# A sparse-attention and feed-forward kernel: a new order table, half products for a third of batch 0, and queries of batches 2 and 3 loaded eight tokens to a partition

## Chip, cores and metric

The kernel runs on one core of a Trainium2 chip. The metric is device time in microseconds (us), the median of several executions. A separate, profiled execution gives the trace that this document reads.

## The reference

The inputs are `q`, `k`, `v` of shape (4 batches, 8 heads, 768 tokens, 64) and the weights of a feed-forward block, all float32. Each query attends to the keys less than 16 tokens away, and to one summary for each block of 32 tokens: the elementwise maximum of the block's keys with the mean of its values, with log 32 added to its score.

```python
k_sum = k.reshape(B, H, nb, block, D).max(axis=3)
v_sum = v.reshape(B, H, nb, block, D).mean(axis=3)
scores_l = scale * q @ k.T            # kept where |i - j| < 16
scores_s = scale * q @ k_sum.T + log(block)
a = softmax([scores_l, scores_s]); attn = a @ [v, v_sum]
h = x @ w_in                          # x: attn as (3072 tokens, 512); h: (3072, 2048)
g = h * sigmoid(beta * h)
out = g @ w_out                       # (3072, 512)
```

## The kernel before

**Tiling.** The four batches are worked one after another, and heads in four groups `g` of two (one head in each half of the 128 partitions). For a group, `kT` and `qn` hold keys and queries transposed: partition = head and feature, free axis = token. A query tile has 64 tokens. Its keys are the 96 in its window and the 24 block summaries, together one 128-column block of `kw`; so one matmul of 64 columns per head and tile gives all its scores (`scores`, L318 to L327: for a group and a half `u` of the tokens, 12 matmuls into two PSUM banks). ScalarE (ACT) takes the exponential of the 768 columns (`weigh`, `e`), VectorE (DVE) multiplies with a band mask (`mask_e`, L338), TensorE (PE) multiplies with the values (`av_mm`, L403; `ve` and `vo` are the values in two alignments, with the block means put in by `vm_all`, L377, and `spread`), and `norm` (L429, L430) divides. The result `xn` is transposed into `xT` by a DMA (`x_dma`, issued on ACT's queue).

**Feed-forward.** The hidden layer has 16 tiles `h_tile` of 128 hidden units: 4 blocks of 128 features times two halves of 384 tokens (L475), then one activation (L488). The first two tiles are opened together over three of the four feature blocks, so that the fourth block of `xT` may come late. The second product (`second_product`) makes two row tiles of 128 tokens at a time by seven half-size products instead of eight (Winograd's form of Strassen's method): `product` (L545) runs 8 matmuls of 256 columns, on operands of which some are sums that DVE makes ahead (`h_sums` of the activations, `w_sums` of the weights), and `gather` adds the parts up and stores. Batch 0 alone uses direct products (`o_atom`, L493): six row tiles of 16 matmuls with 512 columns.

**Order.** Nothing schedules the kernel automatically; every engine runs its instructions in the order in which they are written. `run(main, sides)` goes through a list of PE steps and after step `i` puts in the side steps whose position is below `i + 1`. The stages are, in order: batch 0's attention with the first half of its hidden layer; the second half; batch 0's second product beside batch 1's attention; then for batches 1, 2 and 3 the hidden layer (16 steps, with the next batch's loads, casts and transposes beside it) and the second product (21 steps, with the next batch's attention beside it). Each stage has a list of its own with hand-written positions.

**Loads.** Batches 0 and 1 load keys and queries eight tokens to a partition and turn them on PE. For batches 2 and 3, `hw_load` (L109) loads keys and queries in pieces of 256 bytes, one token of one head each, into one pool `stage` of seven buffers; GpSimd (POOL) casts them to bfloat16 (`kq_cast`, L451, a pool `nat` of five buffers), and `kq_dma` (L455) transposes them into `kT` and `qn` in natural token order. These DMAs, the value loads, `v_odd_dma` (which fills `vo` from `ve`) and most output stores wait their turn on one queue, SyncE's (SP).

The query load and the score matmul before:

```python
nc.sync.dma_start(out=f[:], in_=pair(src, b, g).rearrange("h (j p) d -> p h j d", p=P))
nc.tensor.matmul(s[:, h, j * QT:(j + 1) * QT], kw[g][h * D:(h + 1) * D, m, :], q_tile(g, h, m),
                 start=True, stop=True)
```

Of the kernel before, what the change touches and what calls it, by code (L numbers as in the profile page):

```python
# [8 lines left out]


@with_exitstack
def kernel(
# [43 lines left out]
    stage = ctx.enter_context(tc.tile_pool(name="stage", bufs=7))  # L56
    natp = ctx.enter_context(tc.tile_pool(name="nat", bufs=5))
# [48 lines left out]
    def hw_load(nm, src, b, g):  # L106
        f = stage.tile([P, 2, J6, D], f32, name=nm + "st", tag="st")
        stg[(nm, b, g)] = f
        nc.sync.dma_start(out=f[:], in_=pair(src, b, g).rearrange("h (j p) d -> p h j d", p=P))  # L109
# [210 lines left out]
    def scores(b, g, u, bg):  # L320
        s = big[bg]
        for j in range(HT):
            m = u * HT + j
            for h in range(2):
                nc.tensor.matmul(s[:, h, j * QT:(j + 1) * QT], kw[g][h * D:(h + 1) * D, m, :], q_tile(g, h, m),
                                 start=True, stop=True)
        weigh(b, g, u, s)  # L327
        if g < G - 1 or b == 1:
            mask_e(b, g, u)
# [6 lines left out]
    def mask_e(b, g, u):  # L336
        e = et[(b, g, u)]
        (nc.gpsimd if (b, g) == (1, G - 1) else nc.vector).tensor_mul(out=e.rearrange("p h (m q) -> p h m q", q=QT), in0=e.rearrange("p h (m q) -> p h m q", q=QT),  # L338
# [109 lines left out]
    def kq_cast(eng, nm, b, g):  # L448
        t = natp.tile([P, J6, 2, D], bf16, name=nm + "n", tag="nat")
        nat[(nm, b, g)] = t  # L450
        eng.tensor_copy(out=t[:], in_=stg[(nm, b, g)].rearrange("p h j d -> p j h d"))  # L451

    def kq_dma(nm, b, g):
        t = kT[g][:, W:W + S] if nm == "k" else qn[g][:]
        nc.sync.dma_start_transpose(out=t.rearrange("p (j t) -> p j t", j=J6),  # L455
                                    in_=nat[(nm, b, g)].rearrange("p j h d -> p (j h d)"))
# [13 lines left out]

    def h_part(i, k_lo, k_hi):
        t = big[(i + 2) % 3]
        for kk in range(2):
            for ki in range(k_lo, k_hi):
                nc.tensor.matmul(t[:, kk, 0:HS], w_in_sb[:, ki, i * P:(i + 1) * P],  # L475
                                 xT[:, ki, kk * HS:(kk + 1) * HS], start=(ki == 0), stop=(ki == k1 - 1))

    def h_tile(i):
        t = big[(i + 2) % 3]
        if i > 1:  # L480
            h_part(i, 0, k1)
        elif i == 0:
            h_part(0, 0, k1 - 1)
            h_part(1, 0, k1 - 1)
            h_part(0, k1 - 1, k1)
        else:
            h_part(1, k1 - 1, k1)
        nc.scalar.activation(out=h_sb[:, i, :].rearrange("p (k m) -> p k m", k=2), in_=t[:, :, 0:HS],  # L488
# [385 lines left out]
```

## Time and profile before

| | |
|---|---|
| median of 3 runs | 215.6 us (215.23 to 216.23) |
| profiled execution | 215.75 us, its span 214.0 us |
| PE busy | 201.3 us (94%) |
| DVE / ACT / POOL busy | 137.4 / 117.6 / 65.2 us |
| DMA | 85,274 packets, 34.13 MB, 73,712 packets under 512 B |

The span runs from the first to the last instruction; 1.75 us of the device time lie around it. A busy time is the union of an engine's instructions; matmuls overlap, so a group's mean duration times its count is more than its busy time, and the pace of matmuls is read from a row with many of them in a line. In a row `line engine op out<-in | busy, mean | idle before <-releaser`, the last part tells how long the engine stood idle just before these instructions and what ended that.

### The profile page before, as it was taken

Reading aid. Unit: us, or ns where it says so; the run is one execution under the profiler, and the core shown is the slowest. Engines: PE = TensorE matmul, PEld = TensorE weight load, DVE = VectorE, ACT = ScalarE, POOL = GpSimd, SP = SyncE. Lnnn points to the kernel's source line nnn. Section 1 sums busy time; section 2 is a strip of 40 time slices with the busy share of each in tenths; the row PEclk is TensorE's granted clock in tenths of the full one; section 3 lists DMA queues with packets and bytes.
Section 4 is the critical chain, followed back from the end, with each engine's and each line's share of the span. In section 5 each row is a group of like instructions: output and inputs, shape, how many; then the busy total and the mean of one; then the engine's idle time right before and its main releaser. Section 6 shows DMA issues by size and latency. Waiting matters only on the chain.

```text
span 214.0 us, 5814 instructions
## 1 busy us (share of the span) xinstructions
PE 201.3 (94%) x2414; PEld 140.0 (65%) x2419; DVE 137.4 (64%) x313; ACT 117.6 (55%) x173; POOL 65.2 (30%) x98
## 2 busy tenths in 40 slices
PE   7688999999989999999999989999999999999992
PEld 7567766665535546666877856667778866668881
DVE  5396684797476773898799623898999404465122
ACT  2366776787767106667965027778772157662220
POOL 7808991011432800434230171463301100001011
PEclk9999999999999999999999999999999999999998
DMA  6997999999949987999969999999935720000222
GB/s 117 182 223 130 190 178 189 207 206 214 199 118 206 197 258 178 219 178 198 181 158 241 184 280 193 238 205 191 155 112 72 176 103 0 0 3 0 98 101 98
DMA packets 85274, 34.13 MB, mean 159 GB/s; under 512 B 73712, under 2 KB 82304, under 8 KB 85248
## 3 DMA queue, kind: packets, MB, share of 16 engines
q1 hardware_dynamic: 68192, 24.05, 57.2%
q0 software_dynamic: 7424, 7.34, 21.7%
q10 hardware_dynamic: 9632, 2.37, 7.6%
q8 instruction: 19, 0.31, 0.6%
q14 instruction: 7, 0.06, 0.1%
HBM read 27.37 MB, written 6.29 MB: 157 GB/s over the span
## 4 chain that ended last, share of the span: by engine, by line
PE 61%; DMA 17%; DVE 8%; ACT 4%; POOL 4%; issue 3%; SPq 2%; POOLq 0%; ACTq 0%; DVEq 0%
PE big L475 24%; PE one L545 8%; DMA vst<-in_v_dram 7%; PE one L493 7%; PE acc L545 5%; PE big L461 5%; PE one L467 3%; DMA krow<-in_k_dram 3%; DMA xT<-xn 3%; DMA kst<-in_k_dram 2%; ACT e L334 2%; DVE e L338 2%; POOL ve L343 2%; DMA vo<-ve 2%; PE big L467 2%
## 5 line engine op out<-in xcount | busy, mean ns | idle before, releaser
L475 PE MATMUL big<-xT,w_in_sb 128*128 128x384 bf16 x384 | 63.1, 326 | 0.7 <-DMA xT<-xn 0.7
L488 ACT ACTIVATE h_sb<-big,beta_sb 128x768 bf16<-128x768 f32 x48 | 42.7, 901 | 35.0 <-PE big L475 35.0
L475 PEld LDWEIGHTS <-w_in_sb 128*128 128x128 bf16 x384 | 37.6, 98 | 25.6 <-issue 1.0
L334 ACT ACTIVATE e<-big,bias 128x768 bf16<-128x768 f32 x32 | 27.5, 900 | 7.7 <-PE big L317 4.7
L545 PEld LDWEIGHTS <-h_sb 128*128 128x128 bf16 x288 | 27.4, 98 | 4.1 <-issue 0.2
L545 PE MATMUL one<-w_out_sb,h_sb 128*128 128x256 bf16 x216 | 27.6, 273 | 0.3 <-DVE u L523 0.3
L523 POOL TENSOR_TENSOR o_sb<-p,u 128x256 f32<-128x256 f32 x9 | 6.5, 727 | 67.1 <-DVE u L523 34.4
L523 DVE TENSOR_TENSOR s_sb<-h_sb 128x768 bf16<-128x768 bf16 (+1 forms) x15 | 9.3, 619 | 25.5 <-ACT h_sb L488 25.4
L545 PEld LDWEIGHTS <-s_sb 128*128 128x128 bf16 x216 | 20.5, 98 | 2.8
L493 PE MATMUL one<-w_out_sb,h_sb 128*128 128x512 bf16 x91 | 21.5, 380 | 0.6 <-issue 0.5
L343 POOL CAST ve<-vst 128x832 bf16<-128x832 f32 (+1 forms) x15 | 14.1, 939 | 20.0 <-DMA vst<-in_v_dram 17.6
L523 DVE TENSOR_TENSOR u<-one,p 128x256 f32<-128x256 f32 x18 | 7.5, 419 | 16.8 <-PE one L545 16.7
L338 DVE TENSOR_TENSOR e<-e,mask 128x768 bf16<-128x768 bf16 x22 | 13.5, 631 | 7.0 <-ACT e L334 6.8
L493 PEld LDWEIGHTS <-h_sb 128*128 128x128 bf16 x96 | 8.7, 97 | 10.0 <-issue 0.2
L257 POOL COPY kw<-km 128x288 bf16<-128x288 bf16 x12 | 6.6, 554 | 24.4 <-DVE km L249 12.9
L253 DVE TENSOR_REDUCE km<-kT 128x24 bf16<-128x768 bf16 x12 | 11.2, 944 | 2.4 <-ACT kT L260 2.4
L451 POOL CAST qn<-qst 128x768 bf16<-128x768 f32 x8 | 7.0, 879 | 16.9 <-DMA qst<-in_q_dram 13.9
L430 DVE TENSOR_TENSOR xn<-big,r 128x768 bf16<-128x768 f32 x12 | 11.5, 957 | 0.4
L461 PE MATMUL big<-xT,w_in_sb 128*128 128x384 bf16 x64 | 11.4, 326 | 0.0
L260 ACT COPY p<-one 128x256 f32<-128x256 f32 x9 | 3.3, 368 | 14.0 <-PE one L545 5.4
L698 ACT ACTIVATE h_sb<-big,beta_sb 128x384 bf16<-128x384 f32 x16 | 8.2, 582 | 3.6 <-PE big L461 3.6
L545 PE MATMUL acc<-t_sb,h_sb 128*128 128x256 bf16 x72 | 9.8, 273 | 0.0
(135 smaller groups left out, 308.2 us busy)
## 6 DMA issues: line engine op xcount, KB each, us to landing
out_dram<-o_sb SPq DMA_DIRECT2D x23, 256.0 KB, 3.3
vst<-in_v_dram SPq DMA_DIRECT2D x13, 336.0 KB, 4.9
kst<-in_k_dram SPq DMA_DIRECT2D x8, 384.0 KB, 5.4
qst<-in_q_dram SPq DMA_DIRECT2D x8, 384.0 KB, 4.6
w_in_sb<-in_moe_w_in_dram POOLq DMA_DIRECT2D x4, 512.0 KB, 6.9
w_out_sb<-in_moe_w_out_dram POOLq DMA_DIRECT2D x4, 512.0 KB, 13.9
vo<-ve SPq DMA_DIRECT2D x12, 107.2 KB, 2.9
vst<-in_v_dram SPq DMA_DIRECT2D x3, 416.0 KB, 7.8
```

The source lines that it names most:

```text
L253: nc.vector.tensor_reduce(out=km[g][:, NK:NK + nb], in_=kT[g][:, W:W + S].rearrange("p (n f) -> p n f", f=block), op=ALU.max, axis=AX.X)
L334: nc.scalar.activation(out=e[:], in_=s[:, :, 0:HS], func=ACTF.Exp, bias=bias[:, 0:1], scale=scale)
L338: (nc.gpsimd if (b, g) == (1, G - 1) else nc.vector).tensor_mul(out=e.rearrange("p h (m q) -> p h m q", q=QT), in0=e.rearrange("p h (m q) ...
L343: eng.tensor_copy(out=ve[:, g, lo:hi, 0:D], in_=vst[g][:, lo:hi])
L430: nc.vector.tensor_mul(out=x[:, 3 * us[0]:3 * us[0] + 3 * n].rearrange("p (k j) h d -> p k (j h) d", k=n), in0=tv[:, :, :, 0:D], in1=r[:, ...
L461: nc.tensor.matmul(t[:, 0:HS], w_in_sb[:, ki, i * P:(i + 1) * P], xT[:, ki, 0:HS], start=(ki == 0), stop=(ki == k1 - 1))
L467: nc.tensor.matmul(t[:, 0:HS], w_in_sb[:, ki, i * P:(i + 1) * P], xT[:, ki, lo:lo + HS], start=(ki == 0), stop=(ki == k1 - 1))
L475: nc.tensor.matmul(t[:, kk, 0:HS], w_in_sb[:, ki, i * P:(i + 1) * P], xT[:, ki, kk * HS:(kk + 1) * HS], start=(ki == 0), stop=(ki == k1 - 1))
L488: nc.scalar.activation(out=h_sb[:, i, :].rearrange("p (k m) -> p k m", k=2), in_=t[:, :, 0:HS], func=ACTF.Silu, scale=beta_sb[:, i:i + 1])
L493: nc.tensor.matmul(t[:, 0:hi - lo], h_sb[:, n, ms * P:(ms + 1) * P], w_out_sb[:, n, lo:hi], start=(n == 0), stop=(n == k2 - 1))
L523: eng.tensor_tensor(out=o, in0=a, in1=b, op=op)
L545: nc.tensor.matmul(SLOTS[n], a[:, j, t * P:(t + 1) * P], b[:, j], start=(j == 0 and n not in (2, 3, 7)), stop=(j == J2 - 1), skip_group_ch ...
```

## The change

- **One order table.** All stages from batch 0's first hidden half on are now one list of 158 PE steps, and a table `AT` gives each side step a position in it. Most positions shift by one or two steps, some by more: keys of batch 2 are loaded at 24.3 to 34.7 (before: all four after the seventh direct step), queries of batch 2 from 42.9 on (before: from the start of batch 1's hidden layer), weight sums at 23 to 39 instead of after the direct products.
- **Batch 0.** Row tiles 0, 3, 4 and 1 stay direct; tiles 2 and 5 are made by the seven half products. The operand sums for it (`h_sums` with a column offset) are made in the same stage. All its output copies are on ACT.
- **Four open tiles.** `h_tile(0)` starts tiles 0, 2, 3 and 1 over two feature blocks, then over the third; tile 3 uses the two single banks `one` and has two activations.
- **Attention beside products.** Scores, masks, values have positions of their own; the weighted values of groups 0 and 1 stand together, and those of 2 and 3. All masks are on DVE.
- **Tail.** In the last row tile product 7 comes before 2, and the last store is issued by ACT.
- **Queries of batches 2 and 3.** A load puts 8 successive tokens of one head on a partition (96 partitions, 2 KB runs). The cast has 96 x 1024 elements, the transpose 8 blocks of 96 x 128; `qn` then holds tokens in the order (c, f) for token 8f + c. The score matmul reads 8 runs of 8 columns and writes each run at a stride of 8 words, so that the scores are in natural order again. Keys and queries have pools of their own: 4 and 2 staging buffers, 3 and 2 cast buffers.

```diff
-    stage = ctx.enter_context(tc.tile_pool(name="stage", bufs=7))
-    natp = ctx.enter_context(tc.tile_pool(name="nat", bufs=5))
+    stage = {"k": ...(name="kstage", bufs=4)), "q": ...(name="qstage", bufs=2))}
+    natp = {"k": ...(name="knat", bufs=3)), "q": ...(name="qnat", bufs=2))}
...
+            f = stage[nm].tile([P, 2, 8, D], f32, name="qst", tag="st")
+            nc.sync.dma_start(out=f[0:S // 8].rearrange("p h c d -> p h (c d)"),
+                              in_=pair(src, b, g).rearrange("h (p c) d -> p h (c d)", c=8))
...
-                nc.tensor.matmul(s[:, h, j * QT:(j + 1) * QT], kw[g][h * D:(h + 1) * D, m, :], q_tile(g, h, m),
-                                 start=True, stop=True)
+                o, x = s[:, h, j * QT:(j + 1) * QT], q_tile(g, h, m)
+                if b > 1:
+                    o = o.rearrange("p (f c) -> p c f", c=8)
+                    x = qn[g][h * D:(h + 1) * D].rearrange("p (c f) -> p c f", c=8)[:, :, m * 8:m * 8 + 8]
+                nc.tensor.matmul(o, kw[g][h * D:(h + 1) * D, m, :], x, start=True, stop=True)
...
+    def h_bank(i, kk):
+        if i == 3:
+            return one[kk][:, 0, 0:HS]
+        return big[(i + (2 if i < 3 else 1)) % 3][:, kk, 0:HS]
...
+        if i == 0:
+            for lo, hi in ((0, k1 - 2), (k1 - 2, k1 - 1)):
+                for m in (0, 2, 3, 1):
+                    h_part(m, lo, hi)
+        h_part(i, k1 - 1 if i < 4 else 0, k1)
...
+    main.extend([lambda ms=ms, a=a: o_atom(0, ms, a) for ms in (0, 3, 4, 1) for a in range(4)])
+    products(0, (2,))
     for b in range(1, B):
+        main.extend([lambda i=i: h_step(i) for i in range(k2)])
+        products(b, (0, 1, 2))
...
-                nc.sync.dma_start(out=r[:, DH:], in_=o[:, DH:])
+                nc.scalar.dma_start(out=r[:, DH:], in_=o[:, DH:])
...
+            for n in (6, 5, 2, 7, 3) if t == 0 else (1, 6, 5, 4, 7, 2, 3) if (b, t) == (B - 1, J6 // 2 - 1) else (1, 6, 5, 4, 2, 7, 3):
```

Some rows of the table (steps 24 to 39 are batch 0's direct products, 40 to 46 its half products, 47 to 62 batch 1's hidden layer, 63 to 83 its products, 84 to 120 the same of batch 2, 121 to 157 of batch 3):

```python
    'qt': [26.493, 26.635, 26.868, 27.1],
    'ws': [23.117, 26.262, 39.139, 39.153],      # weight sums
    'hs0': [35.414, 37.183, 43.295, 43.005],     # batch 0's activation sums
    'sc1': [27.654, 27.664, 30.05, 30.06, 31.949, 31.959, 33.471, 33.481],
    'av1': [34.2, 34.866, 36.139, 36.613],
    'ql2': [42.871, 44.703, 53.8, 55.263],       # query loads of batch 2
    'qd2': [53.839, 55.63, 58.673, 64.503],      # their transposes
    'sc2': [64.866, 64.876, 67.93, 67.94, 69.93, 69.94, 70.499, 70.509],
    'av2': [73.131, 73.236, 76.321, 76.684],
    'xd2': [73.35, 76.823, 78.252, 80.767],      # transposes into xT
```

299 lines of the change are left out of this document (155 added, 144 removed).

## The prediction

> **What bounds the kernel now.** I read the page's first part, then a table of busy time by stage, then the list of what the TensorE (PE) waited for, then the timeline at the places that list names.
>
> ```profile
> span 214.0 us, 5814 instructions
> ...
> PE 201.3 (94%) x2414; PEld 140.0 (65%) x2419; DVE 137.4 (64%) x313; ACT 117.6 (55%) x173; POOL 65.2 (30%) x98
> ```
>
> PE is busy for 94% of the span; no other engine passes two thirds. The columns below are: stretch, its length, then busy time of PE, weight loads, DVE, ACT, POOL, then the granted clock and the DMA share.
>
> ```profile
> 49.70:61.40 11.70, 10.18 (x182) 5.68 (x185) 6.50 (x13) 8.76 (x12) 4.13 (x5) 1.00 0.96 196
> 61.40:79.50 18.10, 17.69 (x210) 8.93 (x212) 12.95 (x26) 6.47 (x10) 6.38 (x6) 1.00 1.01 208
> 100.30:124.47 24.17, 23.61 (x390) 19.59 (x388) 18.93 (x45) 13.69 (x24) 4.04 (x7) 1.00 1.16 202
> 146.20:170.50 24.30, 23.68 (x389) 19.65 (x388) 19.86 (x46) 13.69 (x24) 4.08 (x5) 1.00 0.77 141
> 191.50:209.85 18.35, 18.35 (x169) 16.20 (x166) 5.74 (x15) 4.25 (x10) 1.67 (x3) 1.00 0.18 65
> ```
>
> The first two rows are batch 0's second product beside batch 1's attention: PE idles 1.52 and 0.41 us. The next two are the products of batches 1 and 2 beside the next batch's attention: 0.56 and 0.62 us idle. The last is batch 3's product alone, no idle. The clock is full in all. So little PE time is lost between stages, and a change can win only by removing PE work, these idle times, or the tail after 209.85. What PE waited for:
>
> ```profile
> PE big L377 <- POOL ve L343: 0.9, 1, 0.9
> ...
> PE big L475 <- DMA xT<-xn: 0.7, 1, 0.7
> PE big L403 <- ACT e L334: 0.7, 2, 0.4
> ```
>
> One wait for batch 1's values, one of 0.7 us for the last transposed `xT` block at the start of batch 2's hidden layer, and 0.7 us for ACT's exponentials, which is part of the 1.18 us idle in the two product stages.
>
> **The change, part by part.** Durations are those of the profiled execution (span 214.0, device time 215.75 us, so 1.75 us lie around the span). The three timed runs have a median of 215.6; I add the sum to that, and 0.5% of it (1.08 us, about what a measurement can tell from no change) sets the limits 214.52 and 216.68.
>
> *Batch 0's row tiles 2 and 5 by seven half products.* Four of the six row tiles keep 16 matmuls of 512 columns each; the other two share 56 matmuls of 256 columns. The paces are in the chain of waits:
>
> ```profile
> 71.80 7.72 PE one L493 x35
> 79.51 20.80 PE big L475 x128
> ...
> 166.34 1.75 PE acc L545 x16
> ```
>
> 32 x 7.72/35 = 7.06 us go, 56 x 1.75/16 = 6.13 us come: -0.9 us of PE. The price lies on DVE, which now has to make the weight sums and four activation sums (1024 elements each) before these products instead of after. In front of them stand the masks, spreads and norms of batch 1:
>
> ```profile
> L338 DVE TENSOR_TENSOR e<-e,mask 128x768 bf16<-128x768 bf16 x22 | 13.5, 631 | 7.0 <-ACT e L334 6.8 <-issue 0.2
> L430 DVE TENSOR_TENSOR xn<-big,r 128x768 bf16<-128x768 f32 x12 | 11.5, 957 | 0.4
> ...
> L523 DVE TENSOR_TENSOR s_sb<-h_sb 128x768 bf16<-128x768 bf16 x9 | 6.5, 722 | 23.2 <-ACT h_sb L488 23.2
> ...
> L523 DVE TENSOR_TENSOR t_sb<-w_out_sb,t_sb 128x2048 bf16<-128x2048 bf16 x2 | 2.4, 1224 | 0.1
> ```
>
> I followed DVE's new order by hand. Two weight sums (2 x 1.22) now precede the cast of batch 1's first queries, so PE waits some 0.8 us for it. But then PE reaches the sums of `ve` (L377) that much later, and there it waits 0.9 us in any case for the last value cast:
>
> ```profile
> 58.62 2.03 POOL L343 CAST ve<-vst 128x832 bf16<-128x832 f32 x2 [0.84 <-DMA vst<-in_v_dram]
> ```
>
> The value loads are released as before, so the end of that cast stays, and the 0.8 us are hidden; if the values came earlier, the delay would be bare. After it I find new waits of 0.2 (last scores for `big1`), 0.55 (first weighted values for `big1`, whose last exponential is now in front) and 0.7 us (last weighted values behind two norms on DVE), against 0.41 us now. The sums then reach each product 0 to 0.8 us ahead of PE. That is +1.05 us net, and it may be anything from -0.4 to +2.4 (the latter if two 1.22 us sums are late); I take +0.6. Masks of head group 3 leave POOL for DVE, two of 0.63 us, counted above; output copies of batch 0 leave DVE for ACT, which has room (6.47 of 18.10 us).
>
> *Four hidden tiles opened instead of two.* At the start of each hidden layer PE now has 4 tiles x 2 halves x 2 matmuls before it needs `xT` block 2 and 8 more before block 3: 24 x 20.80/128 = 3.9 us in place of 12, 1.95 us. The wait it meets today:
>
> ```profile
> 125.70 1.62 PE L475 MATMUL big<-xT,w_in_sb 128*128 128x384 bf16 x9 [0.74 <-DMA xT<-xn]
> ```
>
> This 0.74 us goes. Next late is ACT: four activations at 0.90 us (one of them split) then follow at PE's pace of 4 x 0.325 us, and the fifth tile waits for the first's bank: 0.325 + 0.2 + 0.9 against 1.3, 0.13 us, three times: +0.4. The 0.2 is my estimate for the hand-over from PE to ACT, from the row above: nine matmuls last 1.62 us where nine paces are 1.46, so a result comes 0.16 us after the next could start. Net -0.3; without cover from PE's 3.9 us the 0.74 returns.
>
> *The order of the attention in the product stages of batches 1 and 2.* The scores of group 3 stand one product earlier, and the weighted values come in two pairs. By ACT's order (eight exponentials of 0.90 us, the table load, five copies) PE's first weighted values still meet about 0.2 us of wait, and 0.1 us remains at the second pair for its masks. Of 0.56 + 0.62 us I take 0.6 as gone; the bounds are 0 and 1.2.
>
> *Tail.*
>
> ```profile
> 209.54 0.77 DVE L523 TENSOR_TENSOR o_sb<-acc,u 128x256 f32<-128x256 f32 x2
> 209.64 0.72 POOL L523 TENSOR_TENSOR o_sb<-p,u 128x256 f32<-128x256 f32 x1 [5.38 <-DVE u L523]
> 210.39 0.33 SPq L567 DMA_DIRECT2D out_dram<-o_sb  x1
> 210.82 0.38 SPq L573 DMA_DIRECT2D out_dram<-o_sb  x1
> ```
>
> The last add ends at 210.31, and its store stands behind another store on SyncE's queue until 210.82. In the new order product 7 comes one product earlier and the last store is issued from ACT's queue, which is empty: -0.4 us (0 to -0.5).
>
> *Queries in 2 KB packets.* Each of the eight loads goes from 1,536 packets of 256 B to 192 of 2 KB.
>
> ```profile
> q1 hardware_dynamic: 68192, 24.05, 57.2%
> ...
> qst<-in_q_dram SPq DMA_DIRECT2D x8, 384.0 KB, 4.6
> ...
> L451 POOL CAST qn<-qst 128x768 bf16<-128x768 f32 x8 | 7.0, 879 | 16.9 <-DMA qst<-in_q_dram 13.9 <-DMA kT<-kn 3.0
> ```
>
> A packet of the first queue costs 0.572 x 214.0 x 16 / 68192 = 28.7 ns of one engine, so the eight loads hold the sixteen engines for 8 x 2.75 = 22 us now; bytes do not change, and I take half of it as saved. On the path that is worth nothing: no PE wait in the list names queries. The casts grow from 768 to 1024 elements per partition (8 x 0.29 us on POOL, which is busy for under half of each hidden layer), and two staging buffers make the third and fourth load wait for the first casts; SyncE then issues them among transposes and value loads, ahead of the products that need them by six products or more (0.87 us each). Taken at 0; the cover gone, a late transpose would cost PE up to its own 4.6 us once a batch.
>
> *Scores of batches 2 and 3.* 192 matmuls of 64 columns now read 8 runs of 8 and write every eighth word of their bank. Now they run like this:
>
> ```profile
> 101.99 0.52 PE L325 MATMUL big<-qn,kw 64*128 64x64 bf16 x24
> 102.45 1.05 PE L545 MATMUL one<-t_sb,s_sb 128*128 128x256 bf16 x8
> ...
> L334 ACT ACTIVATE e<-big,bias 128x768 bf16<-128x768 f32 x32 | 27.5, 900 | 7.7 <-PE big L317 4.7 <-PE big L325 2.9
> ...
> L260 ACT CAST qn<-big 128x768 bf16<-128x768 f32 x4 | 3.2, 800 | 1.3 <-PE big L276 1.3
> ```
>
> 24 in 0.46 us, 19.2 ns each, less than 64 columns at the product's pace (0.109 us / 256 x 64 = 27.3 ns), since the two halves of the array overlap. No matmul here writes with a stride. The nearest rows are ACT's: the cast of the queries reads the same banks at a stride of 128 words and takes 800 ns for 768 elements, the exponential reads in order and takes 900. So the near bound is 0; a gain is excluded, since the columns stay. The far bound is two column times and no overlap, 54.7 ns: 192 x 35.5 ns = 6.8 us. I take 0, the end with a row behind it, and keep the other for the range.
>
> The Trainium skill speaks against that: "PSUM — Partial Sum Buffer", under Specifications, gives 8-byte cachelines and says that an access pattern that is not contiguous slows matmuls significantly. By that rule these scores would run at a lower pace than 19.2 ns allows; no run shown so far has such a matmul, and the rows of ACT, which only reads, do not refute it. It is the first rival.
>
> The sum: -0.9 + 0.6 - 0.3 - 0.6 - 0.4 + 0 = -1.6 us, 214.0 us (214.15 beside the profiled 215.75).
>
> **Rivals.** *Strided score writes at half rate* (the other side). If a column that is written at a stride takes two column times, a score matmul takes 54.7 ns; with the two halves of the array overlapping that is 27.3 ns a matmul (192 x 8.1 ns = +1.6 us), without it 54.7 (+6.8 us). PE is the bound in these stages, so it all lies on the path, but for the 0.3 us of waits a stage that I left standing. The time is 215.6 to 220.8; it turns to slower (216.68) from 33 ns a matmul. For it: no matmul row of this profile writes with a stride, so none shows that the pace holds, and the scores run faster than one half of the array could alone. Against it: ACT's strided read costs nothing. The Trainium skill's rule named above would be this mechanism.
>
> *Sums late on DVE.* In batch 0's stage DVE has 19.45 us of work; four sums of some 0.8 us, a weight sum of 1.22 and two masks of 0.63 make it 25 in 30; if the exponentials come half a microsecond later than I think, the norms push the four sums and the two late weight sums behind their products: up to 2.4 us in place of 0.6, 215.8; with a further lost hand-over to batch 1's hidden layer 216.8.
>
> *All waits go.* If my hand-followed waits are not there: -0.9 - 0.4 - 0.9 (values) - 0.7 - 1.2 - 0.4 - 0.6 (six hand-overs of 0.1 us between kinds of matmul) = -5.1, 210.5. For it: every one of these waits is under 1 us, and orders can move them. Against: the value cast ends when its load lands.
>
> **How the numbers follow.** The forecast's case, 0.43, has its own range 212.5 to 214.9, so 0.35 faster and 0.08 within 0.5%. All waits go: 0.15, faster. Strided writes: 0.32, of which 0.12 within and 0.20 slower. Sums late: 0.10, half within, half slower. Together 0.50 faster, 0.25 within, 0.25 slower. The range 211.0 to 218.6 leaves out the low part of the second case and the dear end of the third.
>
> **What would show it.** Right: the 24 scores of batches 2 and 3 still in about 0.46 us; no wait of L475's successor on `xT`; batch 0's stage 29 to 30 us long; the last store issued by ACT within 0.1 us of its add. Wrong: scores at 33 ns or more; PE waiting for DVE's `s_sb` or `t_sb` before 80 us; a PE wait on `qn`.

## The result: 222.6 us, 3% slower, and the profile after

The changed kernel takes 222.59 us in the median of four runs (220.82 to 223.56), beside 215.69 us for the kernel before in the same session: a ratio of 1.0304, 95% interval 1.0253 to 1.0355. The forecast was 214.0, with 218.6 as the upper end of its range. The profiled execution is the lowest of the four, 220.82 us with a span of 219.1; it shows 5.1 us of the loss, and some 1.8 us lie outside it.

The page of the changed kernel:

```profile
span 219.1 us, 5871 instructions
PE 203.7 (93%) x2443; PEld 144.7 (66%) x2443; DVE 144.3 (66%) x320; ACT 119.1 (54%) x180; POOL 63.1 (29%) x97
...
q1 hardware_dynamic: 57296, 23.92, 51.1%
...
L527 POOL CAST qn<-qst 96x1024 bf16<-96x1024 f32 x8 | 8.7, 1092 | 20.7 <-DMA qn<-qn 18.7
...
qst<-in_q_dram SPq DMA_DIRECT2D x8, 384.0 KB, 5.2
```

The first queue did lose 10,896 packets and 6 points of its share. But the eight query casts on POOL now stand idle 18.7 us for `qn<-qn`, a transpose that must land before a cast buffer is free (before, their wait was 13.9 us for the loads). A loaded query takes 5.2 us to land, not 4.6. What PE waited for, behind the waits of its start (total, times, longest):

```profile
PE one L621 <- DVE s_sb L602: 1.6, 1, 1.6
PE big L556 <- DMA xT<-xn: 1.3, 1, 1.3
PE one L621 <- DVE u L602: 1.3, 1, 1.3
...
PE big L452 <- POOL ve L418: 1.1, 1, 1.1
```

The first three are new in their place: before, the only wait for `xT` was 0.7 us in H2, and the only one for `u` 0.3 us. The stages of the changed kernel, H1, P1, H2 and P2:

```profile
79.89:102.37 22.48, 21.12 (x131) 12.50 (x129) 14.09 (x24) 13.11 (x16) 8.31 (x10) 1.00 1.02 195
102.37:128.54 26.17, 24.78 (x389) 20.93 (x388) 21.05 (x45) 13.69 (x24) 7.25 (x10) 1.00 0.96 176
128.54:149.52 20.98, 20.97 (x131) 12.50 (x128) 13.48 (x22) 13.37 (x18) 7.83 (x9) 1.00 1.05 217
149.52:175.91 26.39, 24.80 (x390) 20.54 (x389) 22.29 (x46) 14.29 (x24) 7.11 (x12) 1.00 0.58 121
```

In each row stand the stretch, its length, the busy time of PE, weight loads, DVE, ACT and POOL, then the granted clock and the DMA share. These stages end where PE starts the first matmul of the next one; H is a hidden layer, P a second product with the next batch's attention, the number is the batch. Read in the same way from the timeline of each kernel, in us:

| kernel | H1 starts | H1 | P1 | H2 | P2 | H3 | P3 | to the end |
|---|---|---|---|---|---|---|---|---|
| before | 79.35 | 20.80 | 24.32 | 21.70 | 24.37 | 20.80 | 18.51 | 4.15 |
| changed | 79.89 | 22.48 | 26.17 | 20.98 | 26.39 | 20.97 | 18.51 | 3.71 |
| changed - before | +0.54 | +1.68 | +1.85 | -0.72 | +2.02 | +0.17 | 0 | -0.44 |

The last row adds up to the 5.1 us. In P1 and P2, PE is busy 24.78 and 24.80 us instead of 23.76 and 23.75, so 2.07 us are more work, and idle 1.39 and 1.59 us instead of 0.56 and 0.62, so 1.80 us are waiting. More work: the scores of batches 2 and 3.

```profile
104.21 0.84 PE L403 MATMUL big<-qn,kw 64*128 64x64 bf16 x24
104.98 1.05 PE L621 MATMUL one<-t_sb,s_sb 128*128 128x256 bf16 x8
```

The product starts 0.77 us after the scores, where it was 0.46. More waiting: two operations of DVE, with what POOL does at that time.

```profile
106.08 3.35 DVE L413 TENSOR_TENSOR e<-e,mask 128x768 bf16<-128x768 bf16 x1 [0.80 <-ACT e L409]
...
148.95 3.84 DVE L602 TENSOR_TENSOR s_sb<-s_sb,h_sb 128x384 bf16<-128x384 bf16 x1
...
98.69 1.06 POOL L527 CAST qn<-qst 96x1024 bf16<-96x1024 f32 x1 [5.03 <-DMA qn<-qn]
99.71 0.74 POOL L331 COPY kw<-km 128x288 bf16<-128x288 bf16 x1
105.10 1.08 POOL L527 CAST qn<-qst 96x1024 bf16<-96x1024 f32 x1 [4.64 <-DMA qn<-qn]
106.13 0.87 POOL L418 CAST ve<-vst 128x832 bf16<-128x832 f32 x1
106.95 0.42 POOL L331 COPY kw<-km 128x288 bf16<-128x288 bf16 x1
107.33 2.85 POOL L418 CAST ve<-vst 128x832 bf16<-128x832 f32 x3
```

A sum of 384 elements takes 0.36 us elsewhere and 3.84 us here; the mask takes 3.35 us instead of some 0.63. Both lie under POOL's run of casts without a pause (105.10 to 110.18, and in the same way 148.70 to 153.5). POOL had stood still for 5.03 and 4.64 us at its third and fourth query cast, with the casts of the values queued behind. In the kernel before the value casts of that stage lie apart, at 96.15, 99.49, 102.57 and 106.35. And H1 has a wait inside:

```profile
74.99 1.42 SPq L181 DMA_DIRECT2D qst<-in_q_dram  x2
...
75.69 1.51 ACTq L517 DMA_TRANSPOSE xT<-xn  x1
...
83.99 0.81 PE L556 MATMUL big<-xT,w_in_sb 128*128 128x384 bf16 x4 [1.34 <-DMA xT<-xn]
```

The last transpose of batch 1's attention is issued right behind two query loads that the table has moved ahead of it, and lands 8.3 us after its issue.

### The profile page after: what moved, and what is told of

It reads as the page before. It is cut to its first block, busy times and chain, and to the rows that moved or that the text cites. A ratio compares the mean times of both kernels' runs of the same rounds, so it can differ in the third digit from the quotient of the medians.

```text
span 219.1 us, 5871 instructions
## 1 busy us (share of the span) xinstructions
PE 203.7 (93%) x2443; PEld 144.7 (66%) x2443; DVE 144.3 (66%) x320; ACT 119.1 (54%) x180; POOL 63.1 (29%) x97
## 4 chain that ended last, share of the span: by engine, by line
PE 42%; DVE 24%; DMA 19%; POOL 5%; issue 4%; ACT 3%; SPq 2%; ACTq 0%; DVEq 0%; POOLq 0%
PE big L556 19%; PE one L621 11%; DMA krow<-in_k_dram 8%; PE acc L621 8%; DVE s_sb L602 6%; DVE e L413 4%; DMA xT<-xn 4%; DMA vst<-in_v_dram 4%; DMA vo<-ve 3%; DVE kw L337 2%; ACT h_sb L568 2%; DVE km L323 2%; DVE t_sb L602 2%; DVE w_out_sb L303 2%; DVE km L327 2%
## 5 line engine op out<-in xcount | busy, mean ns | idle before, releaser
L568 ACT ACTIVATE h_sb<-big,beta_sb 128x768 bf16<-128x768 f32 x45 | 39.6, 904 | 27.8 <-PE big L556 27.7
L621 PEld LDWEIGHTS <-h_sb 128*128 128x128 bf16 x320 | 30.8, 98 | 5.8 <-issue 1.2
L621 PE MATMUL one<-w_out_sb,h_sb 128*128 128x256 bf16 x240 | 30.2, 273 | 1.3 <-DVE u L602 1.3
L602 DVE TENSOR_TENSOR s_sb<-h_sb 128x768 bf16<-128x768 bf16 (+2 forms) x16 | 9.9, 620 | 22.0 <-ACT h_sb L568 22.0
L413 DVE TENSOR_TENSOR e<-e,mask 128x768 bf16<-128x768 bf16 x24 | 16.7, 718 | 3.8 <-ACT e L409 3.6
L334 ACT COPY o_sb<-one 128x256 f32<-128x256 f32 (+1 forms) x14 | 6.0, 430 | 16.9 <-PE one L621 7.9
L572 PE MATMUL one<-w_out_sb,h_sb 128*128 128x512 bf16 x64 | 15.2, 380 | 0.0
L527 POOL CAST qn<-qst 96x1024 bf16<-96x1024 f32 x8 | 8.7, 1092 | 20.7 <-DMA qn<-qn 18.7
L602 DVE TENSOR_TENSOR s_sb<-s_sb,h_sb 128x768 bf16<-128x768 bf16 (+2 forms) x16 | 12.8, 798 | 0.5
L621 PE MATMUL one<-t_sb,s_sb 128*128 128x256 bf16 x80 | 10.7, 274 | 1.6 <-DVE s_sb L602 1.6
```

The lines of the kernel that those rows point to most:

```text
L334: nc.scalar.copy(out=o, in_=i)
L413: nc.vector.tensor_mul(out=e.rearrange("p h (m q) -> p h m q", q=QT), in0=e.rearrange("p h (m q) -> p h m q", q=QT), in1=mask[:, None, u * ...
L568: nc.scalar.activation(out=o, in_=t, func=ACTF.Silu, scale=beta_sb[:, i:i + 1])
L572: nc.tensor.matmul(t[:, 0:hi - lo], h_sb[:, n, ms * P:(ms + 1) * P], w_out_sb[:, n, lo:hi], start=(n == 0), stop=(n == k2 - 1))
L602: eng.tensor_tensor(out=o, in0=a, in1=b, op=op)
L621: nc.tensor.matmul(SLOTS[n], a[:, j, t * P:(t + 1) * P], b[:, j], start=(j == 0 and n not in (2, 3, 7)), stop=(j == J2 - 1), skip_group_ch ...
```

## The experiments

Every kernel ran beside the kernel before, whose medians were 216.12, 216.34, 215.98 and 215.99 us in the four sessions. Each ratio is the measured one, with its 95% interval; it differs by up to 0.5% from the quotient of the two medians. Where costs of several kernels are set side by side, they are the ratios taken times 216 us: 6.6 us for the whole change.

### What the strided scores cost

The theory was that a strided write slows the scores; the rivals, that the read in runs does, or that the loss lies elsewhere.

**Queries as before, in the changed kernel** (loads, casts, transposes, scores; the small pools stay):

```diff
-  f = stage[nm].tile([P, 2, 8, D], ...); 2 KB load; casts and transposes of 8 groups; strided scores for b > 1
+  f = stage[nm].tile([P, 2, J6, D], ...); load, casts and transposes of 6 groups; scores in order
```

> The changed kernel with queries of batches 2 and 3 loaded, cast and transposed as before (256 B pieces, natural order, scores that read and write in order); table, pools and all else as changed. Theory 1 (the strided score matmuls cost PE 13 ns each, 2.5 us in all): 24 scores go from 0.78 back to 0.46 us, and the time falls from 222.6 to about 220. Theory 2 (two query cast buffers make POOL's value casts late and bunched, which holds DVE): the long mask and sum operations on DVE (3.4 and 3.8 us) stay, since the buffers stay two. Rival (the new order alone is slow): 222 to 223, nothing moves but the scores' row. Rival (2 KB packets delay the transposes into xT): the 1.3 us wait on xT goes too, 218.5.

218.81 us, ratio 1.0171 (1.0070 to 1.0271). The scores are back at 0.46 us, P2 at 24.28, but P1 takes 27.06:

```profile
PE big L398 <- DMA qn<-qn: 1.7, 1, 1.7
...
PE big L398 <- POOL kw L326: 1.1, 2, 0.7
```

So by the ratios some 2.9 of the 6.6 us go with the eight-token form (uncertain by about 2 us), and natural queries still come late.

**Writes in order, reads in runs of eight** (which leaves the scores' columns in another order):

```diff
-  o = o.rearrange("p (f c) -> p c f", c=8)
+  o = o.rearrange("p (c f) -> p c f", c=8)
```

> The changed kernel, with scores of batches 2 and 3 that read runs of eight but write in order, so the scores' columns stand in another order than the masks expect; the work is the same. Theory 1 with the write as its cause: 24 scores take 0.46 us, about 220 us. Rival, the read in runs of eight is the cause: 24 scores stay at 0.78 us, 222.6.

**Reads in order, strided writes** (the scores' columns again in another order):

```diff
-  x = qn[g][h * D:(h + 1) * D].rearrange("p (c f) -> p c f", c=8)[:, :, m * 8:m * 8 + 8]
+  x = x.rearrange("p (c f) -> p c f", c=8)
```

> The changed kernel, with scores of batches 2 and 3 that write at a stride of eight words but read 64 columns in order (of queries that are in another order, so the scores are of other queries). The write as cause: 24 scores stay at 0.78 us, 222.6. The read as cause: 0.46 us, 220.

All 288 such matmuls of each kernel, in the list of groups (mean ns of one behind the busy time), first for writes in order, then for reads in order:

```profile
L403 PE MATMUL big<-qn,kw 64*128 64x64 bf16 x288 | 6.8, 191 | 1.4 <-POOL kw L331 1.3
```

```profile
L403 PE MATMUL big<-qn,kw 64*128 64x64 bf16 x288 | 9.3, 225 | 0.1
```

The write is the cause: 9.3 against 6.8 us, and reading in runs costs nothing. Over 192 matmuls that is 13 ns each, 19 to 32 ns. But the time did not follow, though 220 was expected for writes in order: 222.59 us (ratio 1.0307, 1.0189 to 1.0425) with writes in order, 221.9 (no interval) with reads in order. What PE saved it waited, 2.9 us for `u` and 1.3 for `kw`.

**Strided scores alone, in the kernel before:**

```diff
   o, x = s[:, h, j * QT:(j + 1) * QT], q_tile(g, h, m)
+  if b > 1: (o and x rearranged as in the changed kernel)
```

> The kernel before, with only the score matmuls of batches 2 and 3 replaced by the ones that read runs of eight and write at a stride (the queries stay in natural order, so the scores are of other queries). Theory 1: 24 scores take 0.78 instead of 0.46 us, 8 x 0.32 = 2.6 us more on PE, less at most 0.7 us of waits for ACT that PE now reaches later: 217.6 to 218.3. Rival, the cost shows only in the changed order: 215.7.

216.95 us, ratio 1.0041 (0.9996 to 1.0087). More had been expected. In its trace the granted clock is 0.90 in the first 53 us and full behind them; there P1 and P2 take 24.91 us each and PE is never idle. That is 0.59 and 0.54 us more than before: the 0.56 and 0.62 us of waits that stood there have taken up half of the added work. The stride is real, and by itself it is 0.9 of the 6.6 us.

### What the queues behind the queries cost

Theory: POOL, stopped for cast buffers, runs its casts in one go, which holds DVE and then PE. Rival: the order of the table costs by itself.

**A third query-cast buffer:**

```diff
-  "q": ctx.enter_context(tc.tile_pool(name="qnat", bufs=2))
+  "q": ctx.enter_context(tc.tile_pool(name="qnat", bufs=3))
```

> The changed kernel with a third buffer for the query casts (2 KB more). Theory 'GpSimd bunches': GpSimd no longer stops 5.0 and 4.6 us (batch 2), 6.9 and 2.1 us (batch 3) at the third and fourth query cast for a buffer; at most one of the two stops is left, smaller. The casts of the values then run earlier and apart, the two long VectorE operations (3.35 and 3.84 us) fall under 1.5 us, and TensorE's waits for u (1.3) and s_sb (1.6) go: about 219.7 us, 2.9 less than the 222.6 of the changed kernel. Rival 'the order itself is slow': the long operations go, but TensorE finds the next wait right behind and the time stays within 0.7 us of 222.6. Third reading 'writes of the scores are all of it': nothing changes, 222.6, with both long operations still there.

The expectation failed. The runs go from 219.3 to 224.6 us (median 222.84, ratio 1.0315, 1.0235 to 1.0396), and in the trace POOL's stop only has another name:

```profile
96.53 1.04 POOL L527 CAST qn<-qst 96x1024 bf16<-96x1024 f32 x1 [4.06 <-DMA qst<-in_q_dram]
...
103.53 1.07 POOL L527 CAST qn<-qst 96x1024 bf16<-96x1024 f32 x1 [5.28 <-DMA qst<-in_q_dram]
...
147.15 4.67 DVE L602 TENSOR_TENSOR s_sb<-s_sb,h_sb 128x384 bf16<-128x384 bf16 x1
```

Now the third and fourth load are late: they have only two staging buffers, and their place on SP is behind transposes. One short pool had hidden another.

**The first two query loads of batch 2 behind the transposes:**

```diff
-  'ql2': [42.871, 44.703, 53.8, 55.263],
+  'ql2': [47.5, 47.6, 53.8, 55.263],
```

> The changed kernel with the first two query loads of batch 2 issued behind the transposes of batch 1's attention instead of ahead of them (two positions of the table, 42.87 and 44.70, become 47.5 and 47.6). Theory 'the 2 KB loads hold the last transpose': the transpose that took 8.3 us to land lands in 3 to 5 us, TensorE's wait of 1.34 us for xT in the hidden stage of batch 1 goes, and the time is 221.2. Rival 'the transpose was late for another reason' (its own issue time): the wait stays at over 1 us and the time is 222.6. If the casts of the queries start later by as much, the bunch on GpSimd lies later and its cost of 2.9 us may grow; then the time is 222.6 or above with the xT wait gone.

221.43 us, ratio 1.0210 (1.0148 to 1.0273). The wait for `xT` is gone and H1 takes 20.97 us, so the loads had held the transpose. All traces agree: in the eight kernels that issue these two loads ahead of it, in packets of 2 KB or of 256 bytes, this transpose lands 6.1 to 9.2 us after its issue, in the nine others 3.1 to 4.1. P1 grew to 27.00, and its new wait is for the queries:

```profile
114.80 0.85 PE L403 MATMUL big<-qn,kw 64*128 64x64 bf16 x24 [1.79 <-DMA qn<-qn]
```

**Value casts ahead of the third query cast:**

```diff
-  'vc2': [59.6, 64.521, 64.542, 62.062],   'vc3': [95.588, 95.196, 100.009, 100.431],
+  'vc2': [56.0, 56.1, 56.15, 62.062],      'vc3': [90.42, 90.43, 92.5, 100.431],
```

> The changed kernel with three value casts of batch 2 and two of batch 3 put on GpSimd ahead of the third query cast (positions of the table), so that they run while it would stand still for a buffer; the pools stay at two buffers. Theory 'GpSimd bunches': the stop for the third buffer shrinks by the 0.9 us of each cast, the run of casts behind the fourth query cast is 2 to 3 casts shorter, the long VectorE operations (3.35 and 3.84 us) fall under 2 us and 1.5 to 2.9 us come back: 219.7 to 221.1. Rival 'the long operations come from VectorE itself' (its own queue or the wait for a semaphore): they keep their length wherever GpSimd's casts are, and the time stays at 222.6.

220.79 us, ratio 1.0197 (1.0128 to 1.0266). Of the two long operations of DVE none is left (the longest in P1 and P2 takes 1.50 us) and POOL's stop at the third query cast of batch 2 is 0.36 us:

```profile
97.39 1.29 POOL L418 CAST ve<-vst 128x832 bf16<-128x832 f32 x1 [1.52 <-DMA vst<-in_v_dram]
99.03 1.13 POOL L527 CAST qn<-qst 96x1024 bf16<-96x1024 f32 x1 [0.36 <-DMA qn<-qn]
```

So DVE's long operations go with the place of POOL's casts, and do not come from DVE by itself. But a run of casts alone does not make them. With natural queries in the changed kernel POOL works without a pause from 104.45 to 110.62 us, and no operation of DVE in P1 takes over 1.23 us: there the two engines take turns, and one operation of DVE lasts about as long as one cast. Why DVE loses several turns in a row in the changed kernel no run shows. The time is 1.8 us lower by the medians, as expected, but the two intervals overlap, and other waits have come: 2.3 us for `xT` in H1, 1.4 for `qn` in P1, 1.8 for `kw` in P2 (where the granted clock is 0.94).

### The change cut in two

**Everything but the queries and their pools:**

```diff
-  (queries by eight tokens; kstage 4, qstage 2, knat 3, qnat 2)
+  (queries as before; stage 7 and nat 5, shared by keys and queries)
```

> The changed kernel with the queries in every way as before (128-partition loads, casts and transposes of six groups, scores written in order) and with the pools of before, 7 loads and 5 casts shared by keys and queries, 3 KB and 1.5 KB each; what is left of the change is the order, the half products of batch 0, the four open hidden tiles and the tail. Theory 'the query form and the small pools cause the loss': no stop of GpSimd for a query-cast buffer, no VectorE operation over 2 us, the products of batches 1 and 2 take 24.3 us each instead of 26.2 and 26.4, the hidden stage of batch 1 takes 21.0 to 21.7 us instead of 22.5: span 213.1 to 214.4, time 215 to 216. Rival 'the order of the table causes it': with natural queries but two buffers each, the products of batch 1 took 27.1 us; they stay above 26, and the time is 217.5 to 218.8.

**The queries and their pools alone, in the kernel before:**

```diff
-  stage = ... bufs=7; natp = ... bufs=5; queries of six groups; scores in order
+  kstage 4, qstage 2, knat 3, qnat 2; queries by eight tokens; strided scores
```

> The kernel before with only the query part of the change: eight tokens to a partition, casts and transposes of eight groups, strided scores, and pools split in 4 and 2 loads and 3 and 2 casts; order, batch 0, hidden tiles and tail as before. Theory 'the query form and the small pools cause the loss': beside the 0.6 us a batch that strided scores alone cost there, GpSimd stops for query-cast buffers, and the products of batches 1 and 2 take 25.5 to 26.5 us (24.3 before): 218 to 220. Rival 'the order causes it': only the strided scores are seen, 24.9 us a batch, 216.9 as when they alone were put in.

The first takes 218.18 us (ratio 1.0091, 1.0059 to 1.0124), the second 223.64 (1.0349, 1.0321 to 1.0377). The query part alone costs as much as the whole change, 7.5 us; the rest, forecast as a gain, costs 2.0 us. Neither came as expected: the first has the time of its rival, with P1 at 25.82 us and P2 at 23.98, and the second is dearer than 218 to 220. SP's queue in the second kernel shows where it starts:

```profile
83.13 1.32 SPq L465 DMA_TRANSPOSE kT<-kn  x1
89.72 0.32 SPq L112 DMA_DIRECT2D qst<-in_q_dram  x1
90.09 1.22 SPq L465 DMA_TRANSPOSE kT<-kn  x1
...
99.15 1.21 SPq L465 DMA_TRANSPOSE qn<-qn  x1
```

From 84.45 to 89.72 SP stands at the third query load: its staging buffer is free only after POOL's first query cast, which starts at 88.33. That cast stands behind POOL's fourth key cast, which waited 13.80 us for one of the three key-cast buffers. In the kernel before, with five buffers for all, the fourth key cast ran at 74.40, and the third load was issued at 85.77. Three key transposes, the value loads and all four query transposes stand behind it on SP.

**The pools alone, with natural queries:**

```diff
-  stage = ... bufs=7; natp = ... bufs=5
+  kstage 4, qstage 2, knat 3, qnat 2   (3 KB and 1.5 KB each)
```

> The kernel before with only the pools split as in the change (4 and 2 loads, 3 and 2 casts, natural 3 KB and 1.5 KB buffers); queries loaded, cast, transposed and scored as before. Theory 'two query buffers each are too few': the sync queue stands still at the third query load until a query cast has run, GpSimd stops some 10 us at the third query cast, and the products of batches 1 and 2 take 26 to 27.3 us each (24.3 before; 27.8 with the whole query part, of which 0.6 belongs to the strided scores): 219.5 to 222. Rival 'the eight-token form does it': within 0.5 us of the kernel before, 215.5 to 216.5.

**The eight-token form with shared pools of about the same bytes:**

```diff
-  stage = ... bufs=7; natp = ... bufs=5; queries of six groups; scores in order
+  stage = ... bufs=5; natp = ... bufs=4   (4 KB and 2 KB each); queries by eight tokens; strided scores
```

> The kernel before with the eight-token queries and the strided scores, but with pools shared by keys and queries as before, cut to 5 loads and 4 casts for the space (4 KB and 2 KB each). Theory 'two query buffers each are too few': a shared buffer comes free with each key cast, so the third query load and cast wait little, and the time is 216.9 to 218 (the strided scores alone gave 216.9). Rival 'the eight-token form does it' (longer casts, 1.04 to 1.1 us, and transposes of eight groups that land later): 221 to 224, as with the split pools.

221.02 us (ratio 1.0235, 1.0162 to 1.0308) with the pools alone, 217.62 (1.0056, 1.0014 to 1.0097) with the form in shared pools, both in the range of the theory on the pools: 5.1 and 1.2 us. Of the two theories the pools are the one that stands. The pools alone:

```profile
87.31 1.02 POOL L451 CAST kn<-kst 128x768 bf16<-128x768 f32 x1 [14.48 <-DMA kT<-kn]
...
89.13 0.39 SPq L109 DMA_DIRECT2D qst<-in_q_dram  x1
...
102.44 0.83 POOL L451 CAST qn<-qst 128x768 bf16<-128x768 f32 x1 [12.19 <-DMA qn<-qn]
...
PE big L325 <- DMA qn<-qn: 4.0, 5, 1.0
```

and the form in shared pools, where the third load is issued at 84.94 and POOL stands still for about 1 us ahead of the third query cast:

```profile
84.94 0.58 SPq L112 DMA_DIRECT2D qst<-in_q_dram  x1
...
92.98 1.04 POOL L460 CAST qn<-qst 96x1024 bf16<-96x1024 f32 x1 [1.02 <-issue]
...
97.28 2.92 DVE L533 TENSOR_TENSOR s_sb<-h_sb 128x768 bf16<-128x768 bf16 x1
```

What is left there, 1.2 us, has the strided scores in it and a sum that takes 2.92 us instead of 0.55, under a run of casts from 96.73 to 99.78. (These pools have two staging buffers and one cast buffer fewer than before; natural queries in such pools were not run.) No kernel with the 2 KB packets was faster than the kernel before.

Two things are to be read from these kernels. First, the split counts too few buffers for the keys as well as for the queries, and no run takes the two apart. In the shared pools POOL's first query cast comes as late as with the split (88.20, after 13.24 us of wait for a cast buffer), and yet the third load goes out in time; so that late cast alone is not the price. Second, where the query part or its pools stand alone, no operation of DVE behind 75 us takes over 1.31 us: PE waits there for `qn` (2.3 and 4.0 us), `xT` (1.4 and 1.5) and `ve`, not for a long operation of DVE.

In the new order the same parts weigh otherwise. From the changed kernel down, natural queries take 2.9 us off, the pools of before another 1.7, and 2.0 are left (each uncertain by some 2 us). A part of this change has no price that holds in both orders. The stages of these kernels, as in the table above:

| kernel | H1 | P1 | H2 | P2 |
|---|---|---|---|---|
| before | 20.80 | 24.32 | 21.70 | 24.37 |
| everything but the queries | 20.98 | 25.82 | 20.98 | 23.98 |
| queries and pools alone | 20.80 | 27.80 | 22.47 | 27.76 |
| pools alone | 20.80 | 26.42 | 22.60 | 27.13 |
| eight-token form, shared pools | 20.80 | 25.27 | 20.80 | 26.00 |

### Where the rest loses

**Third and fourth query load earlier, in the kernel with everything but the queries:**

```diff
-  'ql2': [42.871, 44.703, 53.8, 55.263],   'ql3': [84, 84.1, 88.62, 90.458],
+  'ql2': [42.871, 44.703, 47.7, 48.7],     'ql3': [84, 84.1, 84.7, 85.7],
```

> The order-only kernel (queries and pools as before) with the third and fourth query load of batches 2 and 3 moved up in the table to 0.7 and 1.7 steps into the hidden stage, where the kernel before has them (47.7, 48.7 and 84.7, 85.7 instead of 53.8, 55.3 and 88.6, 90.5); no other engine's order changes. Theory 'late loads hold GpSimd, which then runs its casts in one go': GpSimd's stops of 5.5 and 4.9 us at the third and fourth query cast shrink to under 2 us, the products of batch 1 fall from 25.8 to 24.1 to 24.5 us, and the span from 215.3 to 213.6 to 214.0. Rival 'the casts stand late in the table by themselves' (positions 56.2 and 59.0 instead of 56.0 and 57.5, and the fourth transpose behind the products' start): the fourth stop goes but the products of batch 1 stay above 25.3.

The runs spread from 216.4 to 221.0 us (ratio 1.0163, 1.0090 to 1.0237), so the time decides nothing. In the trace the stops at both casts are gone, but P1 did not fall (26.57 us): the value casts still stand in a row, only earlier, and now DVE's sums lie under them. They take turns with the casts: sums of 384 elements last 0.92 to 1.03 us instead of 0.36.

```profile
101.38 1.23 DVE L597 TENSOR_TENSOR h_sb<-h_sb 128x768 bf16<-128x768 bf16 x1
...
102.85 2.90 POOL L413 CAST ve<-vst 128x832 bf16<-128x832 f32 x3
...
103.14 0.92 DVE L597 TENSOR_TENSOR s_sb<-s_sb,h_sb 128x384 bf16<-128x384 bf16 x1
...
106.67 0.28 PE L616 MATMUL one<-t_sb,s_sb 128*128 128x256 bf16 x1 [2.28 <-DVE s_sb L597]
```

So late loads were not the whole reason: the table's positions for the value casts (59.6, 62.1 and two at 64.5, where the list before had them 1.2 apart) make a run as well. P2, on the other hand, takes 23.47 us with PE never idle, 0.90 less than before.

**The same kernel as the first of the two halves, with the first two query loads of batch 2 late:**

```diff
-  'ql2': [42.871, 44.703, 53.8, 55.263],
+  'ql2': [47.5, 47.6, 53.8, 55.263],
```

> The first kernel of this call (order, batch 0, hidden tiles and tail of the change; queries and pools as before) with the first two query loads of batch 2 behind the transposes of batch 1's attention. If its hidden stage of batch 1 still waits for xT, that wait (up to 0.7 us) goes and the stage takes 20.97; if the queries come too late for the scores then, a wait for qn of up to 1.8 us stands in the products of batch 1 instead, as it did when this was tried in the changed kernel. Best case: span 213.1, time 214.8, a ratio of 0.996.

219.22 us, ratio 1.0134 (1.0094 to 1.0175): no gain. H1 had no wait there, and P1 grew to 28.00: 1.87 us of it are a wait for `kw`, which POOL copies behind the later query casts (another 1.37 stand in P2), and about 1.5 us come of PE's matmuls, which ran at a granted clock of 0.94 in that stage.

### The parts that gain

**Four open tiles in all batches, and the last store on ACT, in the kernel before:**

```diff
+  h_bank, h_part, h_tile of the changed kernel
-  nc.sync.dma_start(out=r[:, DH:], in_=o[:, DH:])
+  nc.scalar.dma_start(out=r[:, DH:], in_=o[:, DH:])
```

> The kernel before with two parts of the change alone: four hidden tiles held open to the last groups of xT instead of two, and the last half store issued by ScalarE. Theory 'these two parts do what the comparison of the stages showed' (hidden stage of batch 2 0.7 us shorter, tail 0.45 us shorter): 1.2 us less than the kernel before, 214.5 where that has 215.7, and up to 0.7 more if the wait in the hidden stage of batch 1 goes too. Rival 'the shorter hidden stage came from the new order of the attention steps': only the tail's 0.45 is gained, 215.2. Slower than before if the fourth tile, in the two single banks, waits for their last reader of the stage ahead: above 216.

216.31 us, ratio 1.0012 (0.9976 to 1.0049): no gain. H2 takes 20.97 us instead of 21.70, as expected. But where there is no wait to hide the four open tiles cost 0.17 us (H3 20.97 instead of 20.80; H1 took 21.09), and the tail stayed at 4.26 us: the two last stores are now issued within 0.05 us of each other.

```profile
210.73 0.39 ACTq L575 DMA_DIRECT2D out_dram<-o_sb  x1
210.78 0.33 SPq L569 DMA_DIRECT2D out_dram<-o_sb  x1
```

**Four open tiles in batch 2 alone, and both tail edits, in the kernel before:**

```diff
-  run([lambda i=i: h_tile(i) for i in range(k2)], s)
+  run([lambda i=i, f=h_tile if b == 2 else h_tile_old: f(i) for i in range(k2)], s)
-  (1, 6, 5, 4, 2, 7, 3)
+  (1, 6, 5, 4, 7, 2, 3) if (b, t) == (B - 1, J6 // 2 - 1) else (1, 6, 5, 4, 2, 7, 3)
+  nc.scalar.dma_start(out=r[:, DH:], in_=o[:, DH:])
```

> The kernel before with the four open hidden tiles in batch 2 alone (where its profile has the 0.7 us wait for xT) and with both tail edits (the last tile's product 7 ahead of 2, and the last half store issued by ScalarE). Theory 'these are the parts of the change that gain': hidden stage of batch 2 20.97 instead of 21.70, from TensorE's last matmul to the end 3.7 us instead of 4.15: 1.2 us, a ratio of 0.9945. The kernel with the ScalarE store but the old order had a tail of 4.26, so a tail of 3.7 here gives the gain to the order of the last products; a tail of over 4.1 says that it hangs on something else.

214.65 us, ratio 0.9941 (0.9911 to 0.9972), faster than both kernels, and than the kernel before by the amount expected: 1.3 us, 0.6%. H2 takes 20.97 us, and from PE's last matmul (207.89) to the end of the span (211.6) it is 3.7 us:

```profile
123.55:144.52 20.97, 20.95 (x130) 12.51 (x128) 13.50 (x21) 13.12 (x16) 11.36 (x14) 1.00 1.22 222
...
207.55 0.33 SPq L589 DMA_DIRECT2D out_dram<-o_sb  x1
...
207.98 0.38 SPq L599 DMA_DIRECT2D out_dram<-o_sb  x1
208.38 0.38 ACTq L595 DMA_DIRECT2D out_dram<-o_sb  x1
```

With both edits the stores are set apart and the tail is shorter; the other queue alone did nothing. The order of the last products alone was not run.

## Why the prediction was wrong

- **Queries, taken at 0: the step that failed.** The forecast saw that two staging buffers make the third and fourth load wait, and set them "ahead of the products that need them by six products or more". It did not follow what stands behind them: on SP three key transposes, the value loads and the query transposes, on POOL the value casts. Nor did it count the cast buffers, three for keys and two for queries; for the latter POOL stopped 18.7 us in the changed kernel. The query part cost 7.5 us in the order before (5.1 with the small pools alone) and 4.6 in the new one (6.6 less the 2.0 of the rest). The price it named without cover, 4.6 us a batch, was of this size, though that figure is the landing of a load and was put down to a transpose. The sign it named, a PE wait on `qn`, is not in the changed kernel's list: there the cost came by the scores and by DVE under POOL's casts.
- **POOL's casts as harmless** ("busy for under half of each hidden layer"): under a run of them single DVE operations took 3.35 and 3.84 us, and PE waited 1.26 and 1.59 us behind these. The Trainium skill, "SBUF — State Buffer", section "Who interferes with whom", says that a DVE instruction with two SBUF inputs contends with a GpSimd instruction that reads SBUF, and that the pair of ports they share is an exclusive lock. The traces agree: the operations that grew have two such inputs, and sums with one input in PSUM kept their 0.41 us beside such casts (the kernel with natural queries, at 105.61). In some traces DVE and POOL take turns; in the changed kernel one DVE operation stayed blocked over several casts.
- **Scores, taken at 0.** Mis-sized: 32 ns a matmul instead of 19, 2.5 us of PE's work. The rival had the mechanism; its two prices, 27.3 and 54.7 ns, lie on both sides. By itself the stride cost 0.9 us, so this rival would have been inside the range, and it alone does not make the 222.6. The rule of the Trainium skill quoted there, "PSUM — Partial Sum Buffer", under Specifications, agrees with the trace for the write (9.3 against 6.8 us). The operand lies in SBUF, which that line does not speak of, and reading it in runs cost nothing.
- **Attention's order, -0.6.** Not to be seen in the changed kernel: PE's idle time in P1 and P2 rose from 1.18 to 2.98 us, by the waits for `u` and `s_sb`. With the queries and pools of before P2 idles 0.43 us instead of 0.62, and not at all with the loads earlier, while P1 idles 2.17 instead of 0.56. So the gain was there in P2, and in P1 other waits stood in its place.
- **Four open tiles, -0.3.** The 0.74 us of H2 went as said (-0.72, with the 0.17 us that the tiles cost included). "No wait on `xT`" was wrong for batch 1: query loads that the table moved ahead of the transpose made a new one, 1.34 us. That belongs to the order, not to the form of the queries: natural loads in that place made waits of 0.57 and 0.67 us, and in one kernel none. The text had the earlier loads in its list of the change and never asked what they stand in front of.
- **Batch 0, -0.3.** From its first matmul the stage takes 30.00 us (29.64 before), at the edge of "29 to 30"; over the ten traces with the half products it takes 29.4 to 30.6, over the seven without 28.5 to 29.9. The half products take 6.12 us of PE, 6.13 as forecast. Five of the 96 direct matmuls are missing in the trace of before; in the traces that have them all PE is busy 28.3 to 28.5 us with direct products and 27.7 with the half products, so 0.6 to 0.8 us of work went and not 0.9. Two waits are new, 0.53 us for `e` and 0.31 for `xn`, followed by hand as 0.55 and 0.7; taking only 0.6 for all delays was too little. PE did not wait for the sums, so that rival falls.
- **Tail, -0.4.** Measured -0.44; the last store is issued by ACT 0.04 us after its add (215.84, 215.88).
- **All waits go.** This rival falls too: new waits came. No run shows the 0.1 us a hand-over in its sum.

The parts do not add up: 7.5 for the queries alone and 2.0 for the rest, 6.6 together. Each of the three kernels issues the third query load late (89.72, 91.67 and 92.61 us; before 85.77), so they may share one wait, which no run shows. Inside the query part, 5.1 (pools) and 1.2 (form with its strided scores, in shared pools) make 6.3 of 7.5, which these intervals do not tell from a plain sum. Why the rest costs 2.0 us is known only in part: its P1 is 1.50 us longer, and earlier loads did not mend that.

## What to carry to other kernels

When a tile grows, count for every pool how many buffers are left, and follow each in-order queue past the first instruction that now waits: the price is in what stands behind it. Casts that have to wait come in a run afterwards, and a run on GpSimd can hold VectorE. Take a change apart before it is taken or left: here 1.3 us of gain, in small edits, were hidden under a loss of almost 7.

## What was not expected of the hardware

- A score matmul of 64 columns whose fp32 output is written at a stride of eight words takes 32 ns instead of 19; reading its bf16 operand in runs of eight costs nothing.
- A 384-element sum on VectorE took 3.84 us, and 4.67 in two other kernels, instead of 0.36, while GpSimd ran casts without a pause; beside other such runs it took 0.92 to 1.03.
- A transposing DMA took 8.3 us to land when two loads of 384 KB were issued 0.7 us ahead of it on another queue; 6.1 to 9.2 us in eight kernels with these loads ahead, 3.1 to 4.1 in nine without.
